# An attention kernel's order of work: one p·v block for two tiles, and stack parts ahead of weight conversions

## The chip, the cores and the metric

The kernel runs on one core of a Trainium2 chip. The metric is the device time of one execution in microseconds (us). A core has a matrix engine, TensorE (PE; its weight loads are shown apart, as PEld), three other compute engines, VectorE (DVE), ScalarE (ACT) and GpSimd (POOL), and SyncE (SP), which issues the DMAs here. Each engine, and each DMA queue, takes its instructions in the order in which the program gives them.

## What is computed

Three layers follow one another. First an attention with a mask by hash buckets, over 2 batches of 8 heads, 768 positions and 64 dimensions:

```python
q_bits = (np.einsum('bhsd,dk->bhsk', q, proj) > 0)      # the same for k
mask = q_bucket[:, :, :, None] == k_bucket[:, :, None, :]
scores = np.where(mask, scale * np.matmul(q, k.transpose(0, 1, 3, 2)), -1e9)
attn = np.exp(scores - scores.max(-1)); attn = attn / (attn.sum(-1) + 1e-09)
return np.matmul(attn, v)
```

Its output, as 1536 tokens of 512 features, goes through a mixture of 8 experts with room for 192 tokens each (the largest gate values are served first), and that output through a normalisation and a gated layer of width 1536 (`silu(xn @ w_gate) * (xn @ w_val) @ w_out`). The three weight matrices of that last layer arrive as 64-bit floating-point bit patterns and must be turned into float32 on the chip.

## The kernel before

The kernel has three stages: attention (to about 300 us), the choice of experts (to about 345 us), then experts and gated layer. Only the attention stage is touched by the change.

The heads are worked in 8 **pairs** (`NPAIR`), two heads of one batch at a time. A pair has 6 tiles of 128 queries (`TPB`), and each tile has one **unit** per head, so a pair is a window of 12 units and the stage 96 units (`NU`). One unit u of the loop issues, in this order:

- `expo(u+1)`: ACT takes the exponential of the scores (L350) of the next unit.
- `transp(u)`: PE transposes the 128x768 probabilities in six pieces (L361). They are moved out of PSUM in two halves. The second goes over ACT (L363), the first over DVE (L365), except in every fourth unit, where it goes over ACT too.
- `scores(u+2)`: four matmuls (L336, L339) on the stacked parts of q and k, then on DVE a minimum over the row (L341) and two small steps (L342, L343) that give `expo` its scale and bias.
- `comb(i)` and `comb_v(i)` for an earlier tile, in even units: a matmul with the heads' output rows (L395) and its scaling on DVE (L417 to L424).
- `rinv(i)`: the inverse of the sum of the exponentials, on DVE (L404, L405).
- `pv(i, part)`: probabilities times v for tile i = u//2 - 1. The two heads write the two halves of one PSUM tile `xo`, in matmuls 64 columns wide. The even unit does the first three chunks of 128 keys (part 0), the odd unit the last three (part 1), and then ACT moves the result out (L385).
- the **fill** of the unit, a list of other steps that `at(u, f, ...)` has put there.

Two kinds of work stand in the fills. The first makes the **parts** of the next pair. `prep_t` transposes q or k on PE (L278), ACT moves it out (L282, L284), and POOL splits it into a high and a low part (L285, L286). `prep_d` sends six DMAs that stack these parts for `scores` (L310 to L312). `prep_p` makes the hash bits with six matmuls (L294) and a comparison on DVE (L297), and `prep_s` sends these by four small DMAs (L320) into the same stacks. `scores` of the next pair's first unit, issued two units before that pair begins, needs all of it. `load_pair` follows with the loads of the pair after. `SLOTS` names the six units of these steps, counted from the pair's first unit: four for `prep_t`, two for `prep_p` (`SLOTS1` for the first pair).

The second kind is the **conversion** of the 36 weight blocks of 128x512. `conv_load` fetches one (L242), `conv` takes its low words over ACT (L250), its high words over DVE in two steps (L253, L254), and joins them in four steps on POOL (L255 to L258); `conv_store` writes the result to DRAM (L263). Block n has its conversion in unit 5 + n*12//5, so five in every 12 units at an even spacing.

`ps_s` has two buffers of scores in PSUM, `ps_m` three for transposes, hash bits and `comb`, and `ps_v` one for `xo`. The tile framework adds the waits; the order on each engine is the program's order.

Of the kernel before, what the change touches and what calls it, by code (L numbers as in the profile page):

```python
# [9 lines left out]
F32 = mybir.dt.float32  # L10
# [6 lines left out]
AF = mybir.ActivationFunctionType  # L17
# [6 lines left out]
BIG = 2.0 ** 30  # L24
ACT_EVAC = 1
SLOTS1 = (0, 0, 4, 5, 5, 6)
CONV = 5
SLOTS = (-1, 0, 1, 3, 5, 6)
WSTEP = (4, 7, 9, 10, 10, 13, 15, 16)
POOL_LO = (0, 1, 4, 5, 7)  # L30
DVE_HI = (0, 4)
# [15 lines left out]
def lsh_attention__moe__swiglu_kernel(ctx, tc, q, k, v, proj, m_wg, m_w1, m_w2,  # L47
                                      f_wg, f_wv, f_wo, f_g, out):
    nc = tc.nc
# [6 lines left out]
    TPB = S // 128  # L56
# [5 lines left out]
    NPAIR = B * HP  # L62
# [22 lines left out]
    wk = att.enter_context(tc.tile_pool(name="wk", bufs=2))  # L85
    cv = att.enter_context(tc.tile_pool(name="cv", bufs=2))
    ps_s = att.enter_context(tc.tile_pool(name="ps_s", bufs=2, space=PSUM))
    ps_v = att.enter_context(tc.tile_pool(name="ps_v", bufs=1, space=PSUM))
# [17 lines left out]
    def chunk(p, j):  # L106
        return j if p == 0 else 2 * (j % (TPB // 2)) + j // (TPB // 2)
# [119 lines left out]
    convs = []  # L227
    for src, dst in ((f_wg, wg_d), (f_wv, wv_d), (f_wo, wo_d)):
        n = src.shape[0] * src.shape[1] // (128 * 512)
# [93 lines left out]
    SC, PR, PTT, RS, XO = {}, {}, {}, {}, {}  # L323
# [22 lines left out]
    def expo(u):  # L346
        i, h = divmod(u, 2)
        rs, ps = RS[i], SC.pop(u)
        pt = wk.tile([128, 2, HALF], F32, name="pr", bufs=3)
        nc.scalar.activation(pt, ps[:, :, :HALF], AF.Exp, scale=rs[:, h, 1:2], bias=rs[:, h, 2:3],  # L350
                             accum_out=rs[:, h, 3:4])
        PR[u] = pt

    def transp(u):
        pt = PR.pop(u).rearrange("p a b -> p (a b)")
        o = wk.tile([128, TPB, 128], F32, name="pt", bufs=4)
        for half in range(2):
            t = ps_m.tile([128, 512], F32, name="m")[:, :HALF].rearrange("p (c k) -> p c k", c=3)
            for i in range(3):
                c = half * 3 + i  # L360
                nc.tensor.transpose(t[:, i, :], pt[:, c * 128:(c + 1) * 128], ident)  # L361
            if half == 1 or u % 4 < ACT_EVAC:
                nc.scalar.activation(o[:, 3 * half:3 * half + 3, :], t, AF.Copy)  # L363
            else:
                nc.vector.tensor_copy(o[:, 0:3, :], t)  # L365
        PTT[u] = o

    def pv(i, part):
        p = i // TPB
        vt = LD["v", p]  # L370
        if part == 0:
            if i < NU // 2 - 1:
                XO[i] = ps_v.tile([128, 128], F32, name="xo")
            else:
                XO[i] = ps_s.tile([128, 2, 512], F32, name="sc")[:, 0, :128]
        xo = XO[i]
        a = (PTT[2 * i], PTT[2 * i + 1])
        for c in range(3 * part, 3 * part + 3):
            for h in range(2):
                nc.tensor.matmul(xo[64 * h:64 * h + 64], vt[:, h, chunk(p, c), :], a[h][:, c, :],  # L380
                                 start=(c == 0), stop=(c == TPB - 1))
        if part == 1:
            del PTT[2 * i], PTT[2 * i + 1]
            xt = wk.tile([128, 128], F32, name="xt", bufs=3)
            nc.scalar.activation(xt, xo, AF.Copy)  # L385
            XO[i] = xt

    XS = {}

# [2 lines left out]
    def comb(i):  # L392
        p, t = divmod(i, TPB)
        pc = ps_m.tile([128, 512], F32, name="m")
        nc.tensor.matmul(pc[:, :2 * W], XO.pop(i), cb[:, p % HP, :], start=True, stop=True)  # L395
        PC[i] = pc
# [3 lines left out]
    def rinv(i):  # L400
        rs = RS.pop(i)
        ri = wk.tile([128, 2, 2], F32, name="ri", bufs=2)
        for h in range(2):
            nc.vector.tensor_scalar(ri[:, h, 0:1], rs[:, h, 3:4], 1e-9, None, op0=OP.add)  # L404
        nc.vector.reciprocal(ri[:, :, 1:2], ri[:, :, 0:1])  # L405
        RI[i] = ri
# [101 lines left out]
    NU = NPAIR * TPB * 2  # L508
    fill = {}

    def at(u, f, *a):
        fill.setdefault(u, []).append((f, a))

    for p in range(1, NPAIR):
        u0 = (p - 1) * TPB * 2
        slots = iter(SLOTS if p > 1 else SLOTS1)
        for nm in "kq":
            for half in range(2):
                n = u0 + next(slots)
                at(n, prep_t, p, nm, half)  # L520
            at(n, prep_d, p, nm)
        for half in range(2):
            n = u0 + next(slots)
            at(n, prep_p, p, half)
        at(n, prep_s, p)
        if p + 1 < NPAIR:
            at(n + 1, load_pair, p + 1)
    for n in range(len(convs)):
        u = CONV + n * 12 // 5
        at(u - 5, conv_load, n)  # L530
        at(u, conv, n)
        at(u + 3, conv_store, n)
    for i in range(8):
# [67 lines left out]
    for u in range(NU + 3):  # L601

        if u + 1 < NU:
            expo(u + 1)
        if u < NU:
            transp(u)
        if u + 2 < NU:
            scores(u + 2)
        if u == NU:
            rinv(u // 2 - 1)  # L610
            pv(u // 2 - 1, 0)
            pv(u // 2 - 1, 1)
        if u % 2 == 0 and u >= 4:
            comb(u // 2 - 2)
            comb_v(u // 2 - 2)
        if u % 2 == 1 and 3 <= u < NU:
            rinv(u // 2 - 1)
        if 2 <= u < NU:
            pv(u // 2 - 1, u % 2)
        for f, a in fill.pop(u, []):  # L620
            f(*a)
    assert not fill
# [690 lines left out]
```

## Time and profile before

| | us |
|---|---|
| median of three runs | 816.4 (815.01 to 816.46) |
| the profiled execution, its own time | 814.53 |
| its span, first to last instruction | 812.7 |
| PE busy in the span | 761.3 |
| DVE, ACT, POOL busy | 513.7, 398.0, 328.6 |

The profiled execution is 1.9 us under the median, and 1.8 us of its time lie outside the span. PE is busy for 94% of the span, but a busy PE is not a PE at its peak, since the ends of matmuls are modelled: how far apart two steps start is read from the weight loads (PEld). A row of the timeline gives the start, the duration, the engine, the line, the operation with output and input, the number of instructions, and in brackets the idle time before it with what ended it. An `issue` there stands for time in which the engine waited for nothing that the profile shows.

### The profile page before, as it was taken

How to read it: one execution, taken by the hardware profiler on the slowest of the kernel's cores; microseconds unless marked ns; L12 is line 12 of the kernel's file. 1: busy time of each engine (PE TensorE's matmuls, PEld its weight loads, DVE VectorE, ACT ScalarE, POOL GpSimd, SP SyncE). 2: the span in 40 equal slices, each digit the busy share in tenths (PEclk: the TensorE clock that was granted, in tenths of full speed). 3: DMA queues.
4: the chain of work that ended last, by engine and by line, in shares of the span. 5: the costliest groups of instructions: out<-in, count | busy, mean ns of one | idle time of the engine just before them, and what ended most of it. 6: DMA issues, size and time to landing. Idle time of an engine off the chain costs nothing.

```text
span 812.7 us, 14759 instructions
## 1 busy us (share of the span) xinstructions
PE 761.3 (94%) x5317; PEld 685.2 (84%) x5317; DVE 513.7 (63%) x1342; ACT 398.0 (49%) x863; POOL 328.6 (40%) x309
## 2 busy tenths in 40 slices
PE   7999999999989983698999999999999999999997
PEld 3788777787878863498999999999999999999996
DVE  7788786889878878467787887766422332233222
ACT  3677765676766762265676776644211221121111
POOL 3278786877868720586767660000100010001001
PEclk8999999999999995699999999999999999999999
DMA  3578897989879612377777834363200110001001
GB/s 79 175 206 217 258 248 208 271 253 278 213 233 268 192 34 78 96 226 226 244 255 241 261 102 156 117 195 117 78 1 1 40 39 1 1 1 40 1 1 39
DMA packets 89770, 115.58 MB, mean 142 GB/s; under 512 B 22124, under 2 KB 68188, under 8 KB 89692
## 3 DMA queue, kind: packets, MB, share of 16 engines
q1 hardware_dynamic: 87612, 108.28, 44.8%
q0 software_dynamic: 1920, 6.29, 2.1%
q8 instruction: 44, 0.72, 0.4%
q14 instruction: 34, 0.28, 0.1%
q10 hardware_dynamic: 160, 0.00, 0.0%
HBM read 77.62 MB, written 18.87 MB: 119 GB/s over the span
## 4 chain that ended last, share of the span: by engine, by line
PE 37%; issue 18%; POOL 1%; DVE 1%; ACT 1%; POOLq 0%; ACTq 0%; DVEq 0%
PE pg L1194 6%; PE pv L1194 6%; PE py L1029 6%; PE po L1222 6%; PE ph L1005 6%; PE py L1031 3%; PE ph L1007 3%; POOL out_dram L1230 1%; PE ph L983 1%; PE py L1101 0%; DVE wl L218 0%; PE px L1061 0%; PE px L1084 0%; ACT bt L1015 0%; DVE yn L1091 0%
## 5 line engine op out<-in xcount | busy, mean ns | idle before, releaser
L1230 POOL DMA_INDIRECT out_dram<-ot,oi x12 | 11.7, 974 | 307.8 <-DVE ot L1228 306.2
L350 ACT ACTIVATE pr<-sc,rs 128x768 f32<-128x768 f32 x96 | 94.9, 989 | 50.4 <-DVE rs L343 31.6
L341 DVE TENSOR_REDUCE rs<-sc 128x1 f32<-128x768 f32 x96 | 91.5, 953 | 34.7 <-PE sc L339 34.2
L218 POOL TENSOR_TENSOR wl<-wr,wh 128x1024 fp32r<-128x1024 f32 x39 | 95.0, 2446 | 44.0 <-PE ph L983 20.9
L1203 DVE TENSOR_TENSOR a<-sg,pg 128x384 f32<-128x384 f32 x48 | 26.6, 553 | 103.1 <-ACT sg L1201 103.1
L361 PE MATMUL m<-ident,pr 128*128 128x128 f32 x576 | 83.4, 281 | 3.1 <-ACT pt L363 2.5
L380 PE MATMUL xo<-pt,ld_v 128*64 128x128 f32 x1128 | 82.9, 282 | 0.0
L1005 PE MATMUL ph<-xg,wh 128*128 128x384 f32 x256 | 75.3, 363 | 3.8 <-DVE ht L1022 3.1
L1029 PE MATMUL py<-ht,wh 128*128 128x384 f32 x256 | 76.7, 364 | 0.0
L361 PEld LDWEIGHTS m<-ident,pr 128*128 128x128 f32 x576 | 63.8, 141 | 15.1 <-issue 7.4
L380 PEld LDWEIGHTS xo<-pt,ld_v 128*64 128x64 f32 x1128 | 60.0, 137 | 18.6 <-issue 11.9
L1201 ACT ACTIVATE sg<-pg 128x384 f32<-128x384 f32 x48 | 23.5, 490 | 105.8 <-PE pg L1194 105.7
L1207 ACT ACTIVATE ah<-a 128x384 fp32r<-128x384 f32 x48 | 25.2, 525 | 99.3 <-DVE a L1204 99.3
L1194 PE MATMUL pg<-xh,gl 128*128 128x384 f32 x192 | 64.6, 336 | 0.0
L1194 PE MATMUL pg<-xl,gh 128*128 128x384 f32 x192 | 64.5, 336 | 0.0
L1194 PE MATMUL pg<-xh,gh 128*128 128x384 f32 x192 | 64.5, 336 | 0.0
L1194 PE MATMUL pv<-xh,vl 128*128 128x384 f32 x192 | 64.4, 335 | 0.0
L1194 PE MATMUL pv<-xl,vh 128*128 128x384 f32 x192 | 64.4, 335 | 0.0
L1194 PE MATMUL pv<-xh,vh 128*128 128x384 f32 x192 | 64.4, 335 | 0.0
L1031 PE MATMUL py<-ht,wl 128*128 128x192 f32 x256 | 63.7, 253 | 0.0
L215 ACT ACTIVATE wh<-wr 128x1024 fp32r<-128x1024 f32 x50 | 51.2, 1054 | 14.2 <-PE py L1029 11.4
L339 PE MATMUL sc<-s_k,s_q 82*128 82x384 f32 x192 | 49.9, 341 | 8.7 <-DMA s_q<-sg 8.7
(252 smaller groups left out, 1952.4 us busy)
## 6 DMA issues: line engine op xcount, KB each, us to landing
wr<-in_moe_w_dram SPq DMA_DIRECT2D x64, 512.0 KB, 4.7
w<-in_moe_w_gate_dram SPq DMA_DIRECT2D x12, 512.0 KB, 6.4
w<-in_moe_w_val_dram SPq DMA_DIRECT2D x12, 512.0 KB, 5.7
w<-in_moe_w_out_dram SPq DMA_DIRECT2D x12, 512.0 KB, 5.3
s_k<-nh_k SPq DMA_DIRECT2D x28, 192.0 KB, 3.4
s_q<-nh_q SPq DMA_DIRECT2D x28, 192.0 KB, 4.2
ld_v<-in_v_dram SPq DMA_DIRECT2D x8, 384.0 KB, 6.2
wg_d<-ha SPq DMA_DIRECT2D x12, 256.0 KB, 5.5
```

What stands on the lines that cost most here:

```text
L215: nc.scalar.activation(WH[i], WR[i], AF.Copy)
L218: (nc.gpsimd if pool else nc.vector).tensor_tensor(WL[i], WR.pop(i), WH[i], op=OP.subtract)
L339: nc.tensor.matmul(ps[:, n, :HALF], q2[:64 + NS, h, qs], k2[:64 + NS, h, n * HALF:(n + 1) * HALF], start=False, stop=True)
L341: nc.vector.tensor_reduce(rs[:, h, 0:1], ps[:, :, :HALF], axis=AX.XY, op=OP.min)
L350: nc.scalar.activation(pt, ps[:, :, :HALF], AF.Exp, scale=rs[:, h, 1:2], bias=rs[:, h, 2:3], accum_out=rs[:, h, 3:4])
L361: nc.tensor.transpose(t[:, i, :], pt[:, c * 128:(c + 1) * 128], ident)
L380: nc.tensor.matmul(xo[64 * h:64 * h + 64], vt[:, h, chunk(p, c), :], a[h][:, c, :], start=(c == 0), stop=(c == TPB - 1))
L1005: hi = lambda: nc.tensor.matmul(ph[:, :2 * CAP], wh[:, d], xg[:, d].rearrange("p a b -> p (a b)"), start=(d == 0), stop=(d == KD - 1), ski ...
L1029: hi = lambda: nc.tensor.matmul(py[d][:, :2 * CAP], wh[:, ds], ht[:, f].rearrange("p a b -> p (a b)"), start=(f == 0), stop=(f == KF - 1), ...
L1031: lo = lambda: nc.tensor.matmul(py[d][:, :CAP], wl[:, ds], ht[:, f, 0], start=False, stop=False, skip_group_check=True)
L1194: nc.tensor.matmul(t[:, :TJ], a[:, d, :], b_[:, d, :], start=(n == 0), stop=(n == 3 * KD - 1))
L1222: nc.tensor.matmul(PO[j][t], a[:, ts], b_, start=(f == 0 and n == 0), stop=(f == KG - 1 and n == 2))
```

## The change

The six slots of `SLOTS` are now -1, 0, 1, 2, 4, 5, so the last three of these steps move a unit earlier. The conversions follow a table for each window of 12 units: four in the first window, five in each of the next three, four in each of the next three, and five in the last. A load is issued five units ahead of its conversion, or one unit after the conversion three blocks earlier, whichever is later. `pv` does all six chunks in the even unit, and `pv_out`, the eviction, stands in the next odd unit behind the exponential. `rinv` is now issued in the even unit, behind `comb_v`.

```diff
--- before.py
+++ after.py
@@ -24,8 +24,11 @@
 BIG = 2.0 ** 30
 ACT_EVAC = 1
 SLOTS1 = (0, 0, 4, 5, 5, 6)
-CONV = 5
-SLOTS = (-1, 0, 1, 3, 5, 6)
+CONV1 = (6, 8, 9, 11)
+CONV5 = (3, 5, 6, 8, 9)
+CONV4 = (3, 5, 7, 9)
+CONVN = (0, 2, 4, 6, 8)
+SLOTS = (-1, 0, 1, 2, 4, 5)
 WSTEP = (4, 7, 9, 10, 10, 13, 15, 16)
 POOL_LO = (0, 1, 4, 5, 7)
 DVE_HI = (0, 4)
@@ -365,25 +368,24 @@
                 nc.vector.tensor_copy(o[:, 0:3, :], t)
         PTT[u] = o
 
-    def pv(i, part):
+    def pv(i):
         p = i // TPB
         vt = LD["v", p]
-        if part == 0:
-            if i < NU // 2 - 1:
-                XO[i] = ps_v.tile([128, 128], F32, name="xo")
-            else:
-                XO[i] = ps_s.tile([128, 2, 512], F32, name="sc")[:, 0, :128]
+        if i < NU // 2 - 1:
+            XO[i] = ps_v.tile([128, 128], F32, name="xo")
+        else:
+            XO[i] = ps_s.tile([128, 2, 512], F32, name="sc")[:, 0, :128]
         xo = XO[i]
-        a = (PTT[2 * i], PTT[2 * i + 1])
-        for c in range(3 * part, 3 * part + 3):
+        a = (PTT.pop(2 * i), PTT.pop(2 * i + 1))
+        for c in range(TPB):
             for h in range(2):
                 nc.tensor.matmul(xo[64 * h:64 * h + 64], vt[:, h, chunk(p, c), :], a[h][:, c, :],
                                  start=(c == 0), stop=(c == TPB - 1))
-        if part == 1:
-            del PTT[2 * i], PTT[2 * i + 1]
-            xt = wk.tile([128, 128], F32, name="xt", bufs=3)
-            nc.scalar.activation(xt, xo, AF.Copy)
-            XO[i] = xt
+
+    def pv_out(i):
+        xt = wk.tile([128, 128], F32, name="xt", bufs=3)
+        nc.scalar.activation(xt, XO[i], AF.Copy)
+        XO[i] = xt
 
     XS = {}
 
@@ -525,9 +527,12 @@
         at(n, prep_s, p)
         if p + 1 < NPAIR:
             at(n + 1, load_pair, p + 1)
-    for n in range(len(convs)):
-        u = CONV + n * 12 // 5
-        at(u - 5, conv_load, n)
+
+    turns = [CONV1] + [CONV5] * 3 + [CONV4] * (NPAIR - 5) + [CONVN]
+    units = [w * TPB * 2 + u for w, t in enumerate(turns) for u in t]
+    assert len(units) == len(convs)
+    for n, u in enumerate(units):
+        at(max(u - 5, units[n - 3] + 1 if n > 2 else 0), conv_load, n)
         at(u, conv, n)
         at(u + 3, conv_store, n)
     for i in range(8):
@@ -602,21 +607,18 @@
 
         if u + 1 < NU:
             expo(u + 1)
+        if u % 2 == 1 and 3 <= u <= NU + 1:
+            pv_out(u // 2 - 1)
         if u < NU:
             transp(u)
         if u + 2 < NU:
             scores(u + 2)
-        if u == NU:
-            rinv(u // 2 - 1)
-            pv(u // 2 - 1, 0)
-            pv(u // 2 - 1, 1)
         if u % 2 == 0 and u >= 4:
             comb(u // 2 - 2)
             comb_v(u // 2 - 2)
-        if u % 2 == 1 and 3 <= u < NU:
+        if u % 2 == 0 and 2 <= u <= NU:
+            pv(u // 2 - 1)
             rinv(u // 2 - 1)
-        if 2 <= u < NU:
-            pv(u // 2 - 1, u % 2)
         for f, a in fill.pop(u, []):
             f(*a)
     assert not fill
```

Lines move by two or three: L380 of before is L382 now, L361 is L364, L336 and L339 are L339 and L342, L395 is L397, L263 is L266, L242 is L245, L310 to L312 are L313 to L315, L320 is L323, L202 is L205.

**PE, units 8 and 9 of the second window.** The rows are the transposes, the scores, `comb` and `pv` of these units. Before:

```order
L361 MATMUL m<-ident,pr 128x128 x6
L336 MATMUL sc<-s_k,s_q 128x384 x2
L339 MATMUL sc<-s_k,s_q 128x384 x2
L395 MATMUL m<-cb,xt 128x144
L380 MATMUL xo<-pt,ld_v 64x128 x6
L361 MATMUL m<-ident,pr 128x128 x6
L336 MATMUL sc<-s_k,s_q 128x384 x2
L339 MATMUL sc<-s_k,s_q 128x384 x2
L380 MATMUL xo<-pt,ld_v 64x128 x6
```

Now:

```order
L364 MATMUL m<-ident,pr 128x128 x6
L339 MATMUL sc<-s_k,s_q 128x384 x2
L342 MATMUL sc<-s_k,s_q 128x384 x2
L397 MATMUL m<-cb,xt 128x144
L382 MATMUL xo<-pt,ld_v 64x128 x12
L364 MATMUL m<-ident,pr 128x128 x6
L339 MATMUL sc<-s_k,s_q 128x384 x2
L342 MATMUL sc<-s_k,s_q 128x384 x2
```

The same matmuls are issued, but the odd unit's six of `pv` have joined the even unit's, and after the odd unit's scores the next unit's transposes follow at once.

**SP, the queue of DMAs between the last parts of q and the loads of the pair after, in the third window.** Before:

```order
L312 DMA s_q<-nl_q 64x2x384
L263 DMA wg_d<-ha 128x512
L242 DMA w_1584<-in_moe_w_val_dram 128x512
L263 DMA wg_d<-ha 128x512
L202 DMA wr<-in_moe_w_dram 128x4x256
L320 DMA s_k<-sg 18x2x384 x2
L320 DMA s_q<-sg 18x2x384 x2
L98 DMA ld_k<-in_k_dram 128x2x384
```

Now:

```order
L315 DMA s_q<-nl_q 64x2x384
L245 DMA w_1602<-in_moe_w_val_dram 128x512
L323 DMA s_k<-sg 18x2x384 x2
L323 DMA s_q<-sg 18x2x384 x2
L205 DMA wr<-in_moe_w_dram 128x4x256
L101 DMA ld_k<-in_k_dram 128x2x384
```

Of the four transfers that stood ahead of the hash bits (two stores, a load, and an expert's weights) one is left.

**POOL, from the parts of the second window on.** The rows are the last two splits of q's parts and the conversions (the first and the last step of each). Before:

```order
L285 CAST nh_q<-nr_q 128x384
L286 TENSOR_TENSOR nl_q<-nr_q,nh_q 128x384
L422 COPY lp<-xs 128x6x16
L255 TENSOR_SCALAR ha<-ha 128x512
L256 TENSOR_TENSOR ha<-ha,eight 128x512
L257 TENSOR_TENSOR ha<-ha,lr 128x512
L258 TENSOR_TENSOR ha<-ha,sg 128x512
L285 CAST nh_q<-nr_q 128x384
L286 TENSOR_TENSOR nl_q<-nr_q,nh_q 128x384
```

Now:

```order
L288 CAST nh_q<-nr_q 128x384
L289 TENSOR_TENSOR nl_q<-nr_q,nh_q 128x384
L424 COPY lp<-xs 128x6x16
L288 CAST nh_q<-nr_q 128x384
L289 TENSOR_TENSOR nl_q<-nr_q,nh_q 128x384
L258 TENSOR_SCALAR ha<-ha 128x512
L259 TENSOR_TENSOR ha<-ha,eight 128x512
L260 TENSOR_TENSOR ha<-ha,lr 128x512
L261 TENSOR_TENSOR ha<-ha,sg 128x512
```

No conversion stands between the two halves of q any more. In this window five conversions, 20 instructions, now follow one another on POOL before the next pair's first split.

## Rows read from the trace of the kernel before

**Rows 1.** The stage by stretches: us, engines' busy time, PE's clock, DMA share, GB/s.

```profile
90.00:126.00 36.00, 32.71 (x295) 27.53 (x293) 27.79 (x81) 24.00 (x55) 28.28 (x30) 0.98 0.91 256
...
198.00:235.00 37.00, 32.96 (x300) 27.79 (x294) 29.53 (x83) 24.45 (x55) 28.63 (x30) 1.00 0.87 251
...
235.00:269.00 34.00, 33.49 (x304) 28.26 (x304) 28.13 (x82) 24.70 (x57) 26.36 (x28) 1.00 0.85 243
...
269.00:296.00 27.00, 27.00 (x263) 22.82 (x264) 23.23 (x79) 20.60 (x46) 14.71 (x15) 1.00 0.31 102
```

**Rows 2.** Waits between 60 and 320 us: who for whom, total, times, longest.

```profile
PEld sc L339 <- issue: 10.4, 6, 3.3
...
PE sc L339 <- DMA s_q<-sg: 8.7, 4, 3.0
```

**Rows 3.** Timeline of PE's weight loads, two units of the last window.

```profile
272.24 0.64 PEld L361 LDWEIGHTS m<-ident,pr 128*128 128x128 f32 x6 [0.17 <-ACT pt L363]
...
273.74 0.64 PEld L380 LDWEIGHTS xo<-pt,ld_v 128*64 128x64 f32 x12 [0.25 <-issue]
...
274.55 0.64 PEld L361 LDWEIGHTS m<-ident,pr 128*128 128x128 f32 x6 [0.17 <-issue]
...
276.30 0.63 PEld L380 LDWEIGHTS xo<-pt,ld_v 128*64 128x64 f32 x12
...
277.10 0.64 PEld L361 LDWEIGHTS m<-ident,pr 128*128 128x128 f32 x6 [0.17 <-issue]
```

**Rows 4.** The same at the stage's end, two blocks of pv together.

```profile
295.87 0.64 PEld L361 LDWEIGHTS m<-ident,pr 128*128 128x128 f32 x6 [0.17 <-ACT pr L350]
...
297.28 1.34 PEld L380 LDWEIGHTS sc<-pt,ld_v 128*64 128x64 f32 x24
...
298.79 0.30 PEld L395 LDWEIGHTS m<-cb,xt 128*128 128x128 f32 x2 [0.17 <-issue]
```

**Rows 5.** Timeline of SP's queue, ahead of the second stall.

```profile
112.39 0.83 SPq L263 DMA_DIRECT2D wg_d<-ha  x1
...
116.22 1.71 SPq L320 DMA_DIRECT2D s_k<-sg  x2
...
117.97 1.59 SPq L320 DMA_DIRECT2D s_q<-sg  x2
```

**Rows 6.** Weight loads of PE, the stall's end.

```profile
123.84 0.30 PEld L339 LDWEIGHTS sc<-s_k,s_q 82*128 82x128 f32 x2 [3.16 <-issue]
```

**Rows 7.** Timeline of DVE, ACT and PE, the exponential's chain in the last window.

```profile
271.29 0.96 DVE L341 TENSOR_REDUCE rs<-sc 128x1 f32<-128x768 f32 x1 [0.72 <-PE sc L339]
...
272.07 0.68 ACT L250 ACTIVATE lr<-w 128x512 int32<-128x512 uint32 x1
...
272.68 0.99 ACT L350 ACTIVATE pr<-sc,rs 128x768 f32<-128x768 f32 x1
...
272.87 0.59 PE L336 MATMUL sc<-s_k,s_q 128*128 128x384 f32 x2
...
273.66 0.48 ACT L363 ACTIVATE pt<-m 128x384 f32<-128x384 f32 x1
...
273.85 0.96 DVE L341 TENSOR_REDUCE rs<-sc 128x1 f32<-128x768 f32 x1
```

**Rows 8.** Timeline of DVE and POOL, a conversion that meets another.

```profile
64.95 1.27 POOL L258 TENSOR_TENSOR ha<-ha,sg 128x512 int32<-128x512 int32 x1
...
65.09 1.43 DVE L253 TENSOR_SCALAR ha<-w 128x512 int32<-128x512 int32 x1
...
66.44 0.72 DVE L254 TENSOR_SCALAR sg<-w 128x512 int32<-128x512 int32 x1
```

**Rows 9.** One line's instructions, duration ns min/median/max: DVE's first conversion step.

```profile
L253 DVE TENSOR_SCALAR ha<-w x36: 406/426/1462, 41.4 to 285.1; 128x512 int32<-128x512 int32 x36
```

**Rows 10.** Timeline of POOL, one conversion's first and last step.

```profile
273.20 0.72 POOL L255 TENSOR_SCALAR ha<-ha 128x512 f32<-128x512 f32 x1 [2.78 <-DVE ha L253]
...
276.48 1.28 POOL L258 TENSOR_TENSOR ha<-ha,sg 128x512 int32<-128x512 int32 x1
```

## The prediction

> **What bounds the kernel now.** I read the stage by stretches first. In the stretches that hold about one window of 12 units each, PE is busy for 33.49 of 34.00 us where nothing goes wrong, DVE for 28.13, ACT for 24.70, POOL for 26.36 [rows 1]. So PE sets the pace, with DVE not far behind. PE's clock is granted in full there (1.00) and falls to 0.98 in one stretch that has a stall. The last stretch has no parts to make and takes 27.00 us.
>
> The list of waits comes next. While the second matmuls of `scores` stand at the head of PE's queue, their weight loads are held for 10.4 us in all; in four of the cases, 8.7 us, the profile names the DMA of q's hash bits [rows 2]. Those are the windows of 36 to 37 us. The queue of SP tells why it is late: at 112.39 a store goes out, then a load, a second store and an expert's weights, and only at 116.22 and 117.97 the hash bits [rows 5]. PE waits until 123.84 for them, 3.16 us [rows 6]. The other windows' lateness has the same place.
>
> The timeline of weight loads shows the third thing, what a unit costs on PE. Two units last from 272.24 to 277.10, which is 4.86 us [rows 3]. The `pv` block of the odd unit has 0.25 us of idle ahead of it and 0.17 behind it, with nothing that releases it: the blocks differ in form from their neighbours, 64 columns against 128. The reader can see at the stage's end what a block of 24 instructions does: its weight loads take 1.34 us in one run, with a single 0.17 behind [rows 4]. A block of 12 takes 0.64 and pays both gaps.
>
> **The change, part by part.** *One block of pv.* Of 47 tiles handled in the loop's regular units, each loses one entry (0.25) and one exit (0.17): 47 x 0.42 = 19.7 us off PE. The tile after the last unit is one block already. No rows speak for less, as long as PE is what is waited for; the new period of a pair of units is 4.86 - 0.42 = 4.44 us.
>
> *The parts earlier.* The last three preparing steps and the sending of hash bits move one unit up, and three of the four transfers ahead of the bits are gone from the queue. The three that went took from 112.39 to about 116.2 with the one that stays, so some 3 us, and a unit earlier is another 2.3 us (half a pair). That exceeds the longest wait, 3.16. On POOL, q's splits no longer stand behind a conversion, which takes 273.20 to 277.76, 4.56 us [rows 10]. So I take all of the 10.4 us away; the bounds are that and nothing. What is late next in those windows is nothing on the DMA side that the trace shows, but the exponential, below. Everything `prep_s` and `load_pair` issue comes earlier with it; the loads meet free buffers, since their readers ended a window ago.
>
> *The eviction of xo* (`pv_out`) now follows the exponential of the odd unit. Its tile is wanted again two units later, more than 4 us, so it costs nothing; the cover is that distance, and without it PE would wait out one eviction. `rinv` moves behind `comb_v`, the same work in the same pair of units: nothing.
>
> *Uneven units.* This is the cost. PE now has a long even unit and a short odd one. From the odd unit's scores to the transposes of the second next even unit, PE has one period and one `scores`: 4.44 + 0.62 (from 272.87 to the end at 273.74 - 0.25) = 5.06 us [rows 3, 7]. In that time must pass: scores to minimum 0.98 (272.87 to 273.85), minimum to exponential 1.39 (271.29 to 272.68), exponential 0.98 (272.68 to 273.66), one eviction 0.48, the next exponential 0.99 [rows 7], and 0.17 to the weight loads that it releases [rows 4]. That is 4.99: it just fits. In every second pair, ACT has a second eviction of 0.48, 0.41 too much. Over 24 such pairs that is 9.8 us as the upper bound and nothing as the lower, where parts give PE other work meanwhile. About half of the pairs have parts, so I take 5.
>
> *Conversions in bunches.* A conversion puts 0.68 (`lr`) on ACT [rows 7] and twice 0.42 on DVE (its first step by the median) [rows 9] into this chain, which has 0.07 to spare. Twelve of the 36, those in units 3 and 5 of six windows, have `prep_t` or `prep_p` beside them on PE, and I cost them at nothing; that cover is PE's work for the parts. For the other 24 the bounds are 0 (one engine's gap takes it) and 0.84 (all of DVE's part is waited for). I take 0.4, under the 0.61 that `lr` alone would leave over, since tables put many of them in odd units, where ACT has a gap: 24 x 0.4 = 9.6.
>
> *Conversions that meet.* At 65.09 DVE starts a step while POOL is in the last step of the conversion before; it takes 1.43 instead of its usual 0.42, ending after POOL's, and the next takes 0.72 beside another POOL instruction [rows 8, 9]. So a meeting costs 1.31. Such a meeting comes once in each of six windows now. In the change, a conversion that follows within one unit, or on a backlog, meets POOL for certain, at 4.56 us each: one in the first window, three (units 6, 8, 9) in each of three windows, 10 in all, so 4 more: 5.2 us as the upper bound, nothing as the lower, and I take half, 2.6. The Trainium skill has a rule that speaks against the bunches here: SBUF — State Buffer, in its section on two separate sides, says that VectorE and GpSimd share one pair of ports as an exclusive lock, which whoever starts first holds for its whole instruction. The trace agrees: DVE's step outlasts what is left of POOL's 1.27 [rows 8]. By that rule alone the four more meetings would count in full and the sum below would be 2.6 us worse; taken as chance overlaps they would count nothing.
>
> *The loads of weights* come as little as three units (some 7 us) ahead of their conversion in the bunches, before five. No wait for them worth a row is there now. I cost them at nothing, covered by three buffers; a late one would hold ACT, and all exponentials behind it.
>
> *Sum.* Gains 19.7 + 10.4 = 30.1. Costs 5 + 9.6 + 2.6 = 17.2. A clean window pays 34.00 - 33.49 = 0.51 of PE idle now for the same kinds of delay [rows 1], seven times 3.6, which the new costs replace. So 30.1 - 17.2 + 3.6 = 16.5 us less. Everything behind the attention stage stays. The profiled execution took 814.5 (its span 812.7 and 1.8 around it), 1.9 under the median, so it would be 798.0; against the median of 816.4 it is **800**.
>
> **The rivals.** *The bits stay late.* DMA engines are already busy for 0.85 to 0.91 of these stretches [rows 1]; the same transfers in fewer microseconds may land later, and the 10.4 would stay. For it: those shares. Against it: the wait follows the order in SP's queue, and the clean stretch has 0.85 without a wait. Time: 19.7 - 13.6 = 6.1 less, 810.
>
> *Everything is hidden.* DVE and ACT fit the bunches in, as their busy times allow (28.13 and 24.70 of what would be about 31). The bound is 30.1 less, 786. Against it: the chain of 4.99 in 5.06.
>
> *Delays add up, and it is slower.* Where a conversion delays the minimum on DVE and then `lr` delays the exponential behind it on ACT, both are paid: 0.84 + 0.61 = 1.45 each. With the upper bounds of the other two costs (9.8 and 5.2, less 3.6), the gains of 30.1 are used up when each of the 24 costs 0.78. Halfway from there to 1.45, at 1.1, the sum is 26.4 + 11.4 = 37.8, and the time 824. For it: even units hold conversions in the middle windows and in all of the last. Against it: the two delays lie partly side by side, and a late unit gives both engines time to catch up. This is where the last window, with five conversions and no parts, would be longer than its 27.00.
>
> **How the numbers follow.** I give the forecast 0.62, late bits 0.12, everything hidden 0.12, slower 0.14. The forecast's own range is 792 to 810, from prices of 0.1 to 0.8 for a conversion. The range over all, 789 to 819, leaves out the extreme of the hidden case and the upper part of the slower one, some 0.2 together. A measurement of this kernel tells apart about 0.2%, 1.6 us. Faster by more than that: the forecast nearly whole, the hidden case and most of the late one, 0.81. Slower: 0.14. Between: 0.05.
>
> **What would show it.** In the profile after, `pv` should come as 24 weight loads in one run, and the odd unit's scores should be followed by transposes with no gap. The waits of `scores` for the DMA of hash bits should be gone, and a window of five conversions should take 32 to 33 us, one of four 31 to 32, the last 27 to 29. New waits should be transposes held by an exponential, and more steps of L256 (L253 of before) that take over 1 us. I would be wrong if PE still waits for a DMA in the first scores of a pair, if the odd-unit gaps reappear elsewhere on PE, or if the windows end no shorter than 34.

## The result: slower, 827.7 us

The changed kernel takes 827.67 us (median of 4, 825.46 to 829.11), beside 816.43 of the kernel before on the same chip: a ratio of 1.0134 with an interval of 1.0103 to 1.0165. The forecast was 800.0 with a range to 819, so the time lies outside it, on the other side. The profiled execution took 827.08 us.

The page of the kernel after has PE at almost the same busy time, over a longer span:

```profile
span 825.2 us, 14699 instructions
...
PE 760.6 (92%) x5317; PEld 693.7 (84%) x5317; DVE 513.9 (62%) x1342; ACT 395.4 (48%) x863; POOL 329.7 (40%) x309
```

The stage by stretches, for after, with the columns of [rows 1]; each stretch is one window of 12 units, the second to the eighth:

```profile
57.00:98.00 41.00, 32.46 (x297) 28.00 (x296) 30.94 (x84) 24.66 (x55) 33.32 (x35) 0.98 0.78 234
98.00:139.60 41.60, 34.97 (x302) 31.05 (x301) 28.68 (x82) 24.37 (x54) 27.97 (x30) 0.91 0.79 221
139.60:180.00 40.40, 36.25 (x305) 32.13 (x304) 28.78 (x89) 24.31 (x55) 27.96 (x30) 0.91 0.79 219
180.00:213.40 33.40, 31.87 (x298) 27.91 (x297) 27.43 (x91) 23.71 (x53) 23.81 (x25) 1.00 0.81 221
213.40:247.30 33.90, 32.60 (x307) 29.13 (x307) 27.51 (x84) 23.65 (x54) 23.09 (x26) 1.00 0.82 232
247.30:280.50 33.20, 31.79 (x299) 28.01 (x298) 25.83 (x80) 23.64 (x53) 23.45 (x26) 1.00 0.84 237
280.50:309.00 28.50, 27.90 (x276) 24.54 (x275) 25.99 (x88) 22.20 (x51) 23.67 (x23) 1.00 0.44 143
```

This table already holds the answer to "where". The three windows with five conversions take 40.4 to 41.6 us, the three with four take 33.2 to 33.9. PE stands idle for 8.5, 6.6 and 4.2 us in the long ones, and in two of them its clock is 0.91.

Window by window, from the start of one window's first exponential to the start of the next's (the eighth ends with the last exponential's start; us, read from ACT's timeline of each kernel, some of the experiments below among them):

| kernel | 1 | 2 | 3 | 4 | 5 | 6 | 7 | 8 | sum |
|---|---|---|---|---|---|---|---|---|---|
| before | 37.0 | 34.7 | 36.5 | 36.6 | 34.5 | 37.1 | 33.8 | 26.8 | 277.0 |
| after | 38.8 | 41.1 | 41.5 | 40.4 | 33.4 | 33.9 | 33.3 | 26.8 | 289.1 |
| slots alone (e2) | 37.0 | 33.6 | 33.6 | 33.5 | 34.2 | 34.5 | 33.6 | 26.5 | 266.6 |
| slots and block (e4) | 37.3 | 33.5 | 33.5 | 33.5 | 34.1 | 34.4 | 33.5 | 26.6 | 266.3 |
| slots and block, more buffers (e11) | 37.3 | 33.5 | 33.5 | 33.5 | 34.1 | 34.8 | 33.5 | 26.5 | 266.8 |
| after, more buffers (e10) | 38.8 | 35.4 | 35.4 | 35.4 | 33.0 | 33.6 | 32.4 | 26.8 | 270.7 |
| after, pair's loads later (e12) | 38.8 | 39.1 | 37.5 | 37.3 | 33.4 | 33.7 | 32.6 | 27.3 | 279.5 |
| fastest (e17) | 36.0 | 32.6 | 32.6 | 32.7 | 33.8 | 32.9 | 32.6 | 26.3 | 259.5 |

After against before: windows 2 to 4 lose 15.2 us, window 1 loses 1.8, windows 5 to 7 gain 4.9. Together that is 12.1 us of loss. The two profiled executions differ by 12.55 us and the medians by 11.2, so nearly all of the loss lies in the attention stage. The windows do not hold the same number of conversions in both kernels: before has 3, 5, 5, 5, 5, 5, 5, 3 of them, after 4, 5, 5, 5, 4, 4, 4, 5.

What PE waits for is the exponential, and the exponential waits in ACT's queue behind a conversion's `lr`, which waits for its weights. The waits of after, 60 to 330 us (who for whom, total, times, longest):

```profile
ACT lr L253 <- DMA w<-in_moe_w_val_dram: 12.6, 6, 5.6
...
ACT lr L253 <- DMA w<-in_moe_w_gate_dram: 9.4, 4, 4.8
...
PEld m L364 <- ACT pr L353: 21.6, 24, 4.8
```

The longest case, in the timeline of all engines. ACT's exponential at 137.65 has had its scale and bias since 132.0; it stands behind `lr`:

```profile
137.08 0.67 ACT L253 ACTIVATE lr<-w 128x512 int32<-128x512 uint32 x1 [5.63 <-DMA w<-in_moe_w_val_dram]
137.09 0.43 DVE L256 TENSOR_SCALAR ha<-w 128x512 int32<-128x512 int32 x1 [5.07 <-DMA w<-in_moe_w_val_dram]
...
137.65 0.98 ACT L353 ACTIVATE pr<-sc,rs 128x768 f32<-128x768 f32 x1
...
138.77 0.93 PEld L364 LDWEIGHTS m<-ident,pr 128*128 128x128 f32 x5 [4.77 <-ACT pr L353]
```

And why the weights are late: SP's queue in after. This conversion is the one of unit 9. Its load is due in unit 6, which on the engines begins near 119 us (the exponential issued in that unit starts at 119.68). SP gets to it at 130.23, behind the hash bits, an expert's weights, the three loads of the next pair and a store, and it lands at 137.08, 6.85 us later:

```profile
125.28 0.77 SPq L323 DMA_DIRECT2D s_q<-sg  x1
126.08 0.47 SPq L205 DMA_DIRECT2D wr<-in_moe_w_dram  x1
126.60 1.49 SPq L101 DMA_DIRECT2D ld_k<-in_k_dram  x1
128.13 0.47 SPq L101 DMA_DIRECT2D ld_q<-in_q_dram  x1
129.25 0.37 SPq L101 DMA_DIRECT2D ld_v<-in_v_dram  x1
129.71 0.41 SPq L266 DMA_DIRECT2D wg_d<-ha  x1
130.23 0.37 SPq L245 DMA_DIRECT2D w<-in_moe_w_val_dram  x1
```

SP also stands long at the send of the next pair's first part, with every later load behind it. Its waits between 57 and 180 us, in after and then in before:

```profile
SPq L313 <- POOL nh_k L288: 35.6, 3, 12.6
...
SPq L310 <- POOL nh_k L285: 31.6, 4, 9.3
```

So this wait is not new. Its longest case has grown from 9.3 us to 12.6; whether the late conversions lengthen it is not shown, since in that case the half of `nh_k` that SP waited for starts at 105.88, released by ACT's eviction of `nr_k`, while POOL's last conversion had ended at 100.61.

The view of DMA issues of the kernel *before*, between 60 and 130 us, had the number that decides this (columns: KB each, median us from issue to landing):

```profile
w<-in_moe_w_gate_dram SPq DMA_DIRECT2D x7, 512.0 KB, 6.4
```

A load took 6.4 us there once issued. The prediction took three units for some 7 us; even at the 33.5 us a window of e4 below they are 8.4 (3 of 12 units), so 2.0 us were left for its place in a queue in which one issue takes 0.4 to 1.5 us.

### The profile page after: what moved, and what is told of

Its sections match the earlier page's. It is cut to its first block, busy times and chain, and to the rows that moved or that the text cites. A ratio compares the mean times of both kernels' runs of the same rounds, so it can differ in the third digit from the quotient of the medians.

```text
span 825.2 us, 14699 instructions
## 1 busy us (share of the span) xinstructions
PE 760.6 (92%) x5317; PEld 693.7 (84%) x5317; DVE 513.9 (62%) x1342; ACT 395.4 (48%) x863; POOL 329.7 (40%) x309
## 4 chain that ended last, share of the span: by engine, by line
PE 36%; issue 18%; DVE 1%; POOL 1%; ACT 1%; POOLq 0%; ACTq 0%; DVEq 0%
PE pg L1196 6%; PE pv L1196 6%; PE py L1031 6%; PE po L1224 6%; PE ph L1007 5%; PE py L1033 3%; PE ph L1009 2%; POOL out_dram L1232 1%; PE ph L985 1%; PE py L1103 0%; DVE wl L221 0%; PE px L1063 0%; ACT bt L1017 0%; PE px L1086 0%; ACT sq L1049 0%
## 5 line engine op out<-in xcount | busy, mean ns | idle before, releaser
L353 ACT ACTIVATE pr<-sc,rs 128x768 f32<-128x768 f32 x96 | 95.2, 992 | 50.3 <-DVE rs L346 33.5
L364 PE MATMUL m<-ident,pr 128*128 128x128 f32 x576 | 87.4, 286 | 23.2 <-ACT pr L353 15.8
L364 PEld LDWEIGHTS m<-ident,pr 128*128 128x128 f32 x576 | 65.3, 144 | 40.4 <-ACT pr L353 23.0
L1205 DVE TENSOR_TENSOR a<-sg,pg 128x384 f32<-128x384 f32 x48 | 26.6, 554 | 102.5 <-ACT sg L1203 102.5
L382 PE MATMUL xo<-pt,ld_v 128*64 128x128 f32 x1128 | 72.8, 279 | 0.0
L382 PEld LDWEIGHTS xo<-pt,ld_v 128*64 128x64 f32 x1128 | 61.5, 138 | 7.0 <-issue 0.5
L339 PE MATMUL sc<-s_k,s_q 128*128 128x384 f32 x192 | 59.2, 391 | 0.0
L366 ACT ACTIVATE pt<-m 128x384 f32<-128x384 f32 x120 | 56.1, 490 | 6.1 <-PE m L364 5.9
```

What stands on the lines that cost most here:

```text
L339: nc.tensor.matmul(ps[:, n, :HALF], q1[:, h, qs], k1[:, h, n * HALF:(n + 1) * HALF], start=True, stop=False)
```

## The experiments

Each kernel ran beside the kernel before on the same chip; ratios are to that, with the 95% interval.

**The parts one by one (e1 to e5).** e1 is before with the block of `pv` alone (the two halves of one tile, not two tiles, in one block; `pv`, `pv_out` and the loop's order of the change). e2 is before with the slots alone:

```diff
-SLOTS = (-1, 0, 1, 3, 5, 6)
+SLOTS = (-1, 0, 1, 2, 4, 5)
```

e3 is before with the conversions' tables and their rule for loads alone. e4 is the changed kernel with the conversions back as they were (`...` marks lines left out, here and below):

```diff
...
-    for n, u in enumerate(units):
-        at(max(u - 5, units[n - 3] + 1 if n > 2 else 0), conv_load, n)
+    for n in range(len(convs)):
+        u = CONV + n * 12 // 5
+        at(u - 5, conv_load, n)
...
```

e5 is the changed kernel with `pv` back in two halves and the loop's old order.

> The kernel before with one part of the change: p*v of a tile in one block, its eviction in the next odd unit. Theory A (the slow windows come from weight loads that are issued too late in SP's queue, an effect of the conversion tables): no conversion waits for its load here, so the block keeps part of its 19.7 us, and 803 to 813 us come out. Theory B (the uneven units are the cause: the exponential is late for the transposes behind the short odd unit): 822 us or more, with the waits of transposes for the exponential at 20 us or more.

> The kernel before with the new slots alone: the next pair's last three preparing steps one unit earlier, conversions as before. Theories A and B both: most of the 8.7 us wait for the hash bits goes, 807 to 813 us; it tells how much of that gain needs the conversion tables too.

> The kernel before with the conversion tables alone, p*v in two halves and the old slots. Theory A: the windows with five conversions have late loads again, ACT waits 15 us or more for them, and the kernel is slower than before, 822 to 834 us. Theory B: the bunches do no harm in even units, 812 to 818 us, with no window over 38 us.

> The changed kernel with the conversions back at their even spacing (one block of p*v and the new slots stay). Theory A: the late loads are gone, and with them the loss: 798 to 810 us. Theory B: the uneven units still hold the transposes, 820 us or more.

> The changed kernel with p*v back in two halves: new slots and conversion tables stay. Theory A (late weight loads make the slow windows; the block only adds to it since there the transposes wait for the exponential anyway): the late loads remain, 814 to 824 us. Theory B (block and tables only hurt together): 803 to 808 us, as with the slots alone.

| | us | ratio | interval |
|---|---|---|---|
| e1 block | 820.08 | 1.0049 | 1.0021 to 1.0077 |
| e2 slots | 803.75 | 0.9852 | 0.9810 to 0.9895 |
| e3 tables | 818.56 | 1.0057 | 1.0023 to 1.0092 |
| e4 slots and block | 804.10 | 0.9852 | 0.9809 to 0.9894 |
| e5 slots and tables | 828.98 | 1.0167 | 1.0122 to 1.0211 |

Three things follow. The slots are worth 1.5% (12 us). The block is worth nothing here: e4 has the ratio of e2, and e5, which has no block, is as slow as the changed kernel within the intervals. The tables cost nearly 3% on top of the slots (1.0134 against e4's 0.9852, 1.0167 against e2's 0.9852), and far less without them (e3). e1 met neither number that was on record: with the bits still late, PE's waits for `s_q<-sg` grew from 8.7 us to 13.0, and a wait for `ld_q` of 11.8 came with it; why the block alone makes these transfers later was not taken apart. e3 met neither of its numbers, e2 gained more than was expected of it, and e5 is slower than either theory had it.

**Are the loads the cause (e6, e7, e10, e11, e12)?** e6 is the changed kernel with five buffers of weights instead of three and loads up to eight units ahead:

```diff
-        w = cv.tile([128, 512], I64, name="w64", bufs=3)
+        w = cv.tile([128, 512], I64, name="w64", bufs=5)
...
-        at(max(u - 5, units[n - 3] + 1 if n > 2 else 0), conv_load, n)
+        at(max(u - 8, units[n - 5] + 1 if n > 4 else 0), conv_load, n)
```

e10 has four such buffers (with n - 4) and six of the result `ha` instead of four. e7 only spaces the conversions in windows 2 to 4, `CONV5 = (2, 4, 6, 8, 10)`. e12 only puts the next pair's loads back into unit 7, where they were before the slots moved:

```diff
-            at(n + 1, load_pair, p + 1)
+            at(n + 2, load_pair, p + 1)
```

e11 is e4 with e10's buffers and loads up to eight units ahead, as a control.

> The changed kernel with five buffers for raw weight blocks instead of three, and each load issued eight units ahead, or one unit after the conversion five blocks earlier. Theory A: the loads stand ahead of the parts in SP's queue, ACT's waits for them fall under 5 us, windows 1 to 3 go back to 33 to 35 us, and 803 to 810 us come out. Theory C (the bunches themselves: ACT's and DVE's conversion steps and the meetings with POOL): the waits for loads go too, but windows 1 to 3 stay at 37 us or more, 816 us or more.

> The changed kernel with five conversions in the second to fourth window in units 2, 4, 6, 8, 10 instead of 3, 5, 6, 8, 9: no two in neighbouring units, every load at least four units ahead. Theory A: loads in time, 802 to 810 us. Theory C: the meetings with POOL go as well, 802 to 810; with e6 it tells which of the two costs, the load or the meeting, is the larger.

> The changed kernel with four buffers for raw blocks, loads eight units ahead or one unit after the conversion four blocks earlier, and six buffers for results in place of four. Theory A, widened (loads and stores both wait in SP's queue behind the parts; with early loads the buffer of a result whose store is late became the wait): no wait of over 2 us for a DMA is left on ACT or DVE, windows 1 to 3 take 34 to 36 us, 802 to 810 us. Theory C (bunches on ACT, DVE and POOL): 37 us or more for these windows, 814 us or more.

> The changed kernel with the loads of the pair after one unit later, in unit 7 as before the change, so that the last raw block of the bunch stands ahead of them in SP's queue. Theory A: that load arrives some 2 to 4 us sooner, most of the longest waits of ACT go, and each of windows 1 to 3 gets 2 us or more shorter: 815 to 823 us. Theory F (the queue's place does not matter, the transfers are slow because the DMA engines are full): 826 to 830 us.

> The kernel of e4 with four raw and six result buffers and loads eight units ahead: a try at the best version. Theory A: only some 1.3 us of waits for loads are left in e4, so 800 to 804 us; if the order of the queue still costs in ways no wait names, below 798.

| | us | ratio | interval |
|---|---|---|---|
| e6 five buffers, earlier loads | 817.74 | 1.0027 | 1.0005 to 1.0050 |
| e7 spaced | 807.99 | 0.9898 | 0.9851 to 0.9945 |
| e10 earlier loads, more results | 807.35 | 0.9900 | 0.9853 to 0.9947 |
| e12 pair's loads later | 817.76 | 1.0041 | 1.0017 to 1.0065 |
| e11 control | 804.30 | 0.9851 | 0.9804 to 0.9899 |

e6 took the wait for loads away and 1.1% of the time (1.0134 to 1.0027), over a third of what the tables cost, and showed the next wait in the same chain: DVE's first step of a conversion now waits for the *store* of an earlier result, whose buffer it needs. By its time, e6 met theory C (816 us or more), which blames the bunches; the waits are why that is not the end of it. Waits of e6, 57 to 170 us:

```profile
DVE ha L256 <- DMA wg_d<-ha: 8.8, 3, 5.4
...
DVE ha L256 <- DMA wv_d<-ha: 2.1, 1, 2.1
```

With more result buffers too (e10), no DMA holds ACT or DVE in these windows, PE's clock is whole, and 2.3% come back, some 19 us. Its second window:

```profile
57.00:92.40 35.40, 32.11 (x297) 27.61 (x296) 32.84 (x84) 24.58 (x56) 32.30 (x33) 1.00 0.74 208
```

Spacing alone (e7) does the same with the old buffers. e12 shows that the queue's order alone is worth 0.9% (1.0134 to 1.0041). The same buffers are worth nothing without the tables (e11). So transfers that come too late are shown as the cause of the loss: the loads first, and behind them the stores that free the result buffers. More result buffers with the old loads were not run, so the shares of 1.1% and 1.3% hold in this order only. What e10 leaves against e11, which has the same buffers and evenly spaced conversions, is the price of the bunches themselves with their transfers in time: 270.7 against 266.8, or 3.9 us for the stage.

**Why is the block worth nothing (e8, e9, e13, e14, e16)?** One window each of e2 and of e4:

```profile
88.80:122.40 33.60, 33.05 (x302) 28.18 (x302) 27.85 (x82) 24.26 (x54) 27.65 (x30) 1.00 0.92 268
```

```profile
89.00:122.50 33.50, 32.06 (x302) 28.44 (x301) 27.70 (x82) 24.05 (x54) 27.65 (x30) 1.00 0.91 265
```

The block takes 1.0 us off PE's busy time in a window, and PE's idle time grows from 0.55 to 1.44. The wait that grows is the transposes' for the exponential: their weight loads are held for 15.1 us in 26 cases between 60 and 300 us in e4, and for 1.3 us in e2. The longest of a window, in the timeline of e4:

```profile
64.74 1.29 PEld L379 LDWEIGHTS xo<-pt,ld_v 128*64 128x64 f32 x24
...
66.20 0.31 PEld L278 LDWEIGHTS m<-ident,ld_q 128*128 128x128 f32 x3 [0.17 <-DVE ri L403]
...
66.79 0.49 ACT L282 ACTIVATE nr_q<-m 128x384 f32<-128x384 f32 x1 [1.80 <-PE m L278]
...
67.17 0.68 ACT L250 ACTIVATE lr<-w 128x512 int32<-128x512 uint32 x1
...
67.75 0.98 ACT L350 ACTIVATE pr<-sc,rs 128x768 f32<-128x768 f32 x1
...
68.87 0.64 PEld L361 LDWEIGHTS m<-ident,pr 128*128 128x128 f32 x6 [1.08 <-ACT pr L350]
```

In an even unit with parts, `prep_t`'s transposes now stand behind 24 of `pv` instead of 12. ACT, in order, waits 1.80 us for them to evict `nr_q`; a conversion's `lr` and the exponential stand behind, and the transposes that need this exponential wait 1.08 us.

To see which part of this chain matters, e8 and e9 are e2 and e4 without ACT's `lr` (POOL adds a tile of zeros, so the low words of the converted weights are left out). e13 and e14 are e2 and e4 with the row minimum over 16 of 768 columns; what follows the attention stage then takes other branches, so only this stage is read. e16 is e4 with `pv` issued behind the unit's parts:

```diff
         if u % 2 == 0 and 2 <= u <= NU:
-            pv(u // 2 - 1)
             rinv(u // 2 - 1)
         for f, a in fill.pop(u, []):
             f(*a)
+        if u % 2 == 0 and 2 <= u <= NU:
+            pv(u // 2 - 1)
```

> The kernel of e2 (new slots, two halves of p*v, even conversions) without ACT's step of a conversion: POOL adds zeros in place of the low words. It is the base for e9. PE is the limit in e2, so both theories expect little: 798 to 804 us.

> The kernel of e4 (the block of p*v added to e2) without that step, likewise. Theory D (the block's 19.7 us are given back where the transposes wait for the exponential on a busy ACT): with 24 us of work off ACT the block shows, 5 us or more below e8. Theory E (the block saves nothing on PE, its gaps come back elsewhere): within 2 us of e8.

> The kernel of e2 with the row minimum taken over 16 of the 768 scores, which makes DVE's step of about 0.96 us short; the softmax is no longer the reference's. It is the base for e14: PE is the limit in e2, so windows stay at 33 to 34 us with both theories. Later stages may branch differently, so the length of the attention stage is what counts.

> The kernel of e4 (block of p*v, new slots, even conversions) with that short minimum, likewise. Theory D, widened (the block does save its time on PE, and the chain from scores over minimum and exponential to the transposes takes it back): with 0.8 us less in the chain the windows fall to 30.5 to 32.5 us, and the last one by 1.5 us or more, below e13's. Theory E (the block saves nothing on PE): the same windows as e13, within 0.5 us.

> The kernel of e4 with the block of p*v issued behind the unit's fill instead of ahead of it, nothing else. Theory G (in even units the next pair's transposes stand behind the long block on PE, ACT's eviction of them waits, and the exponential behind that eviction is late, 0.66 us in unit 2 and 1.08 us in unit 4 of a window): these waits go, the windows with parts fall from 33.5 to 31.5 to 33 us, and 791 to 800 us come out. Theory E (the block saves next to nothing on PE): 802 to 806 us.

Without `lr`: 803.54 us, 0.9849 (0.9803 to 0.9896), and with the block 802.82, 0.9850 (0.9801 to 0.9899), as theory E had it. The transposes' idle time for the exponential over the whole run falls from 15.7 us in e4 to 10.5, and the time hardly moves. With the short minimum (one execution of each) it is 10.5 as well, and windows 2 to 4 are 33.3, 32.9, 33.9 without the block and 33.3, 32.8, 34.2 with it. So in the windows with parts neither of the two is the main cause; ACT's wait for `nr_q` is still there in e14, at 1.79 us.

The last window, which has no parts, says something else. In e4 the block gains nothing there (26.6 us, and 26.5 in e2); with the short minimum it gains 1.1 us (25.7 in e14, 26.8 in e13). The weight loads of e14 there:

```profile
269.91 0.64 PEld L361 LDWEIGHTS m<-ident,pr 128*128 128x128 f32 x6 [0.17 <-issue]
...
271.16 0.76 PEld L361 LDWEIGHTS m<-ident,pr 128*128 128x128 f32 x6
...
274.50 0.64 PEld L361 LDWEIGHTS m<-ident,pr 128*128 128x128 f32 x6 [0.17 <-issue]
```

No transposes of that window wait for the exponential any more, and two units take 4.59 us. So where there are no parts, the chain over the row minimum is what takes the block's gain.

e16 takes most of the transposes' wait for the exponential away, 5.7 us being left, but is slower than e4: 809.04 us, 0.9907 (0.9882 to 0.9933), which neither theory had. The matmuls of the hash bits, now ahead of `pv`, come before their operands. PE's waits for weights in e16, 56 to 290 us:

```profile
PEld m L294 <- POOL ha L255: 9.7, 6, 1.6
PEld m L278 <- ACT pt L363: 5.2, 6, 1.5
PEld m L361 <- ACT pr L350: 5.1, 14, 0.9
```

The profile puts the first down to a conversion's step; what those matmuls read comes from POOL's splits and needs a free tile of PE's output, and how the 9.7 divides between the two was not settled. In e4, `pv` had covered it.

**A version that beats both (e15, e17).** e15 is e4 with three more edits: ACT's extra eviction of `pt` moves from an even unit to an odd one, conversions start in even units only, and a conversion's `lr` and last two POOL steps come one unit later:

```diff
-            if half == 1 or u % 4 < ACT_EVAC:
+            if half == 1 or u % 4 == 1:
...
-        u = CONV + n * 12 // 5
-        at(u - 5, conv_load, n)
+        u = (CONV + n * 12 // 5) // 2 * 2
+        at(max(u - 5, 0), conv_load, n)
         at(u, conv, n)
+        at(u + 1, conv_b, n)
```

where `conv_b` holds `lr` and the additions of `lr` and `sg`. e17 is e15 with e16's edit on top.

> The kernel of e4 with the exponential's chain relieved and all work kept: the second eviction by ACT stands in an odd unit instead of an even one, a conversion's DVE steps are in an even unit and its ACT step in the odd one behind it. Theory D: waits of transposes for the exponential fall under 10 us and 790 to 800 us come out, faster than e2. Theory E: 803 to 806 us.

> The kernel of e15 (second eviction in an odd unit, a conversion's ACT step one unit behind its DVE steps) with the same move of the block. Theory G: 789 to 799 us, at least as fast as e16, the fastest of all. Theory E: within 2 us of e15's 802.6.

e15: 802.57 us, 0.9838 (0.9803 to 0.9874), no better than e4 within the intervals, and between the numbers of the two theories. PE's wait for the exponential falls to 4.2 us, but waits for the evictions of `pt` take its place (8.7 and 6.5). e17: **795.07 us, 0.9745 (0.9684 to 0.9807)**, the fastest here, some 21 us under before and within theory G's numbers. Its windows 2 to 4 are 32.6 to 32.7:

```profile
86.80:119.40 32.60, 31.55 (x302) 28.62 (x300) 30.37 (x82) 24.40 (x54) 27.94 (x30) 1.00 0.90 260
```

PE is idle for 1.05 us there, against e4's 1.44, and 0.5 us less busy. The operands of the hash bits no longer come late: L294 of e16, here L298, waits 1.4 us for POOL, where it was 9.7. So the move of `pv` behind the parts costs about 5 us on e4 and gains about 7.5 on e15: it pays only with e15's edits. Which of the three edits is needed was not taken apart, and no run has them with `pv` in two halves, so how much of the 21 us is the block's own is not shown.

## Why the prediction was wrong

**The step that failed: "The loads of weights".** It read: "I cost them at nothing, covered by three buffers; a late one would hold ACT, and all exponentials behind it." The mechanism was named and its price set to zero. What it measured is about 19 us, with the stores that are late behind the loads: the changed kernel at 1.0134 (1.0103 to 1.0165) against e10 at 0.9900 (0.9853 to 0.9947). Earlier loads alone give back 1.1% (e6). The cover was reckoned in buffers, not in time: three units, less 6.4 us in flight, less the queue. And the edit of the slots, credited with the gain of earlier bits, had put those bits and the pair's loads just ahead of these loads in SP's queue; that was told in the prediction ("the loads meet free buffers") and not followed to who stands behind them. In windows 2 to 4, after takes 123.0 us against e4's 100.5. PE idles there for 19.3 us against 4.8, and is busy for 8.0 us more with the same matmuls (103.7 against 95.7), with a mean clock of 0.93 against 1.00.

This step turned a gain into a loss, but it is half of the miss. Slots and block were to give 25.1 us (30.1 less 5 for the uneven units) and gave 12 (e4). The tables were to cost 8.6 (9.6 and 2.6, less 3.6) and cost 23 (from 0.9852 to 1.0134), 19 of them by the late transfers and 4 by the bunches. The second step that failed is the block, below.

**The bits earlier: right.** Predicted 10.4 us, measured 12 in e2 (interval 8.6 to 15.5). The waits of [rows 2] are gone; in after, L342 waits 0.4 us once. The queue's order, the split on POOL and the earlier unit were not taken apart.

**One block of pv: form right, size wrong.** The 24 loads come in one run and the odd unit's gaps are gone. But the sum gave 0.42 us a pair. Here are two undisturbed units of after, to be held against [rows 3], with the pairs before and behind them:

```profile
286.54 0.64 PEld L364 LDWEIGHTS m<-ident,pr 128*128 128x128 f32 x6 [0.39 <-ACT pr L353]
...
289.76 0.64 PEld L364 LDWEIGHTS m<-ident,pr 128*128 128x128 f32 x6 [0.17 <-issue]
...
291.01 0.79 PEld L364 LDWEIGHTS m<-ident,pr 128*128 128x128 f32 x6
...
292.92 1.29 PEld L382 LDWEIGHTS xo<-pt,ld_v 128*64 128x64 f32 x24
...
294.38 0.64 PEld L364 LDWEIGHTS m<-ident,pr 128*128 128x128 f32 x6 [0.17 <-ACT pt L366]
...
296.21 0.64 PEld L364 LDWEIGHTS m<-ident,pr 128*128 128x128 f32 x6 [0.57 <-ACT pr L353]
```

They last 4.62 us, where 4.86 was and 4.44 was forecast: the transposes straight behind the scores take 0.79 instead of 0.64, and that is most of the 0.18 missing. So the 0.17 of idle behind the odd unit's `pv` was hardly saved, and the 0.25 ahead of it was. The pairs before and behind last 4.88 and 5.04: their transposes wait for the exponential, and so do those in the windows with parts. Of 19.7 us nothing reached the time.

**Uneven units: right in kind, too small.** The chain of 4.99 in 5.06 was the right one to fear. In the last window, where it was read, the wait is there: 0.33 to 0.60 us in four pairs of after, and gone with the short minimum of e14. It was priced at 5, at most 9.8. But most of it, 13.8 of e4's 15.1 us, comes in the windows with parts, which the prediction took for a cover. There the longest cases stand behind the eviction of `nr_q`, which the chain did not have. That this eviction is the main cause there is argued from the timeline: the run that shortens ACT's wait for it (e16, from 1.80 us to 0.55) brings another wait at once. The waits eat what the block gives.

**Conversions in bunches and meetings: too dear.** 9.6 and 2.6 us were put down; e10 against e11 has 3.9 for both. The last window, with five conversions where there were three, takes 26.8 as before. The cover of the sum was not quite as told: of units 3 and 5 only unit 5 has parts beside it, since the new slots leave unit 3 empty. Windows of four take 33.2 to 33.9 us where 31 to 32 was forecast, as the block's gain is not there. DVE's two steps of all conversions, L256 and L257, take 40.9 us in after and 38.9 before: 2.0 more, beside the prediction's bound of 5.2. Nine of these steps take over 1 us, three of L256 and six of L257, and before there were six; none of the nine is in windows 5 to 7. The longest of L256 takes 1.33 us instead of 0.43, from 50.18 us on, while POOL is in a step from 49.94 to 51.22. The Trainium skill's page SBUF — State Buffer, in its section on two separate sides, has a lock between VectorE and GpSimd, for some forms of VectorE's steps, a condition that the prediction left out. The trace agrees with a lock: that step of L256 ends 0.29 us behind POOL's.

**The rival "slower"** had 0.14 and 824 us: the right side and nearly the size, by another mechanism, so its nearness is luck. By its own mark, a last window longer than 27.00, it did not happen. Late bits did not either.

## What to carry to other kernels

When work is bunched, read how long its load takes from issue to landing and what stands ahead of it in the issuing queue, and compare that in us with the distance left; the number of buffers does not say it. An edit that moves transfers earlier makes those behind them later, so follow the queue on to its next reader. And time taken off the busiest engine counted here only where the in-order engine that feeds it was not itself waiting for that engine's work of the same unit.

## What was unexpected of the hardware

PE pays for a stall after it, too. The stall of 134 to 138.7 us in after, by stretches with the columns of [rows 1]:

```profile
126.00:134.00 8.00, 6.59 (x72) 5.73 (x72) 5.50 (x16) 4.03 (x9) 7.21 (x7) 1.00 1.06 274
134.00:138.70 4.70, 0.24 (x6) 0.00 (x0) 1.61 (x4) 1.62 (x4) 1.68 (x3) 0.81 1.04 411
138.70:142.00 3.30, 3.23 (x13) 3.13 (x14) 2.08 (x9) 2.03 (x6) 3.14 (x3) 0.50 0.13 51
142.00:148.00 6.00, 6.00 (x54) 5.65 (x52) 3.19 (x12) 3.73 (x9) 2.41 (x5) 0.85 0.01 3
```

PE was busy for 0.24 us of the 4.70 in which its clock fell; the next 3.3 us ran at 0.50, the lower level of 1.2 GHz, and the full 2.4 GHz came back only within the stretch to 148 us. The DMA engines were full in the stretches before (1.06 and 1.04) and almost empty behind (0.01): so the late load stood in a burst of its neighbours, while the mean over the window was 0.79.

The second surprise is the transposes: the same six loads take 0.64 us behind `pv`, after 0.17 of idle, and 0.79 behind the scores with none. Following at once saved 0.02 us.
